# Attention and experts on one core: two of four steps of a root on ScalarE, three groups without float32 products, and a new order of tasks

## The chip, the cores and the metric

One NeuronCore of a Trainium2 chip runs the whole kernel; the other cores take no part. The metric is the device time of one execution in microseconds (us). A profile comes from one further execution, recorded by the hardware profiler: its span runs from the first to the last instruction and is a little shorter than that execution's device time.

## The reference, cut to what matters

Attention over 8 batches of 12 heads, 448 rows of 64, with normalised queries and keys; its output goes through a mixture of 8 experts with a router that places each token by sorted scores.

```python
rms = np.sqrt(np.mean(x * x, axis=-1, keepdims=True) + 1e-06)   # for q and for k
q_n, k_n = x / rms * g
scores = scale * np.matmul(q_n, k_n.transpose(0, 1, 3, 2))
attn = np.exp(scores - np.max(scores, axis=-1, keepdims=True))
attn = attn / (np.sum(attn, axis=-1, keepdims=True) + 1e-09)
x = np.matmul(attn, v)             # then tokens x 768
logits = x @ w_gate                # greedy: each token to one expert, 448 to an expert
h = np.maximum(x[mask] @ w1[e], 0.0)
out[mask] = h @ w2[e]
```

## The kernel before, in words

**Stages.** Attention comes first (to about 453 us of the profile), then the first search of the router (to about 486 us), then eight experts, whose products fill TensorE to the end. The change touches attention alone.

**Groups.** Four heads make a group, and there are 24 groups (g = 0 to 23). A group has seven blocks of query rows (d = 7 g + b, b = 0 to 6) for each of two halves. Two pairs of results (pair = 2 g + a) come out of a group, 48 in all; six pairs make a batch, which goes on to the router.

**One group's way through the engines.** ScalarE squares q and k (`sq`), VectorE sums the squares (`ss`), then comes the reciprocal square root of the sums (`r`): n = 1 is a logarithm and n = 2 an exponential on ScalarE, and n = 3 is one refinement by Newton's rule, y (y*y*ms - 192) in four small operations on GpSimd, lines 311 to 314, on 28 numbers a partition. Groups 0 and 1 refine on VectorE instead (lines 317 to 319). Then q and k are scaled by the root (`normk` on GpSimd, `normq` on ScalarE in 14 pieces), q is multiplied by the gains (`gain`, GpSimd), both are split in a high and a low float16 part (`hi` on ScalarE, `lo` on GpSimd), and a DMA transposes the parts (`trh`, `trl`).

TensorE then forms products for the row maxima (`max`, line 497), which VectorE reduces (`red`, line 506), and the scores (`score`, lines 528 and 530). ScalarE takes the exponential of a block of scores (`exp`, line 536, into e). TensorE multiplies e with the values (`av`, seven units a pair; the last of the seven in two halves).

**Wide and narrow blocks.** A block of e is either *wide*, one float32 product with the values in float32 (line 571), or *narrow*, three float16 products (lines 577, 579, 581), for which e's low part is first formed by `split` (line 552) on GpSimd, or on VectorE. `MIX` has a letter for each group: "4" has four wide blocks, "2" has two (b = 0 and 4, one in each pair), "0" none. `LO_POOL` names the blocks that are split on GpSimd.

**The end of a pair.** VectorE divides by the sums (`xn0`, `xn1`, `xn2`, lines 603 to 607) and writes the high and low parts (`xhi`, `xlo`, lines 623 to 629); only then is the pair's accumulator free, of which there are two. The logits of batches 0 to 6 are formed by `gate`, copied by `glo` (ScalarE) and added by `gsum` (VectorE); `early` is the first part of the router's work on them, 12 operations on VectorE (lines 1147 to 1187). The last batch is turned on TensorE (`xturn`, line 660, one for each of its pairs), copied out by ScalarE and VectorE (`xtd`, lines 673 and 675) and projected (`glast`), and `gcopy` (line 720) ends the stage.

**Order.** Every task goes to one engine (T TensorE, D VectorE, A ScalarE, P GpSimd, S the DMA queue of SyncE), and every engine works its tasks strictly in the order of the table `ORDER`, two characters a task. The numbers in `US` and the arguments on times and buffers serve the program that made the table and the check of its consistency; they set no order themselves.

## Time and profile before

| | us |
|---|---|
| three runs | 959.23, 955.66, 954.76 |
| median | 955.66 |
| profiled execution, device time | 961.13 |
| its span | 959.4 |
| busy in the span: PE, VectorE, ScalarE, GpSimd | 906.9, 692.6, 512.7, 459.6 |

PE is the name of TensorE in the profile, DVE of VectorE, ACT of ScalarE, POOL of GpSimd. Matmuls overlap in the engine's pipeline, so the busy time of PE says little of its load; the distance from one start to the next does. The profiled execution was 5.5 us longer than the median run.

### The profile page before, as it was taken

Reading aid. Unit: us, or ns where it says so; the run is one execution under the profiler, and the core shown is the slowest. Engines: PE = TensorE matmul, PEld = TensorE weight load, DVE = VectorE, ACT = ScalarE, POOL = GpSimd, SP = SyncE. Lnnn points to the kernel's source line nnn. Section 1 sums busy time; section 2 is a strip of 40 time slices with the busy share of each in tenths; the row PEclk is TensorE's granted clock in tenths of the full one; section 3 lists DMA queues with packets and bytes.
Section 4 is the critical chain, followed back from the end, with each engine's and each line's share of the span. In section 5 each row is a group of like instructions: output and inputs, shape, how many; then the busy total and the mean of one; then the engine's idle time right before and its main releaser. Section 6 shows DMA issues by size and latency. Waiting matters only on the chain.

```text
span 959.4 us, 24827 instructions
## 1 busy us (share of the span) xinstructions
PE 906.9 (95%) x10288; PEld 584.3 (61%) x10288; DVE 692.6 (72%) x1559; ACT 512.7 (53%) x945; POOL 459.6 (48%) x460
## 2 busy tenths in 40 slices
PE   2799999999999999998699999899999999999996
PEld 1367777676777677777466556455565565655553
DVE  6889999998999889884887787577876858234110
ACT  5889988888877888753052424233332424233111
POOL 7779999999988889873100302111112011110001
PEclk9989999999999999999599999999999999999999
DMA  7477889898997979571272919496866739583001
GB/s 190 116 141 144 206 170 207 167 211 156 235 199 168 161 183 167 127 151 60 87 236 90 322 47 243 147 252 185 240 173 212 208 135 285 166 176 124 30 17 42
DMA packets 264229, 157.72 MB, mean 164 GB/s; under 512 B 189876, under 2 KB 251316, under 8 KB 263092
## 3 DMA queue, kind: packets, MB, share of 16 engines
q1 hardware_dynamic: 258674, 133.66, 58.8%
q0 software_dynamic: 4608, 22.02, 7.0%
q8 instruction: 80, 1.31, 0.6%
q10 hardware_dynamic: 834, 0.46, 0.2%
q14 instruction: 33, 0.27, 0.1%
HBM read 94.42 MB, written 22.02 MB: 121 GB/s over the span
## 4 chain that ended last, share of the span: by engine, by line
issue 36%; PE 35%; POOL 14%; DVE 5%; DMA 4%; ACT 3%; POOLq 0%; SPq 0%; DVEq 0%; ACTq 0%
PE po L571 7%; PE psc L528 7%; PE ph L1669 6%; POOL pl L552 4%; PE pm L497 3%; POOL out_dram L1702 3%; POOL rows L1607 3%; PE py L1686 2%; POOL s L376 2%; PE psc L530 2%; DVE mx L506 2%; PE po L577 2%; PE po L581 2%; PE po L579 2%; DMA kq<-s 1%
## 5 line engine op out<-in xcount | busy, mean ns | idle before, releaser
L1669 PE MATMUL ph<-xt,w1h 128*128 128x448 f16 (+2 forms) x804 | 210.9, 345 | 4.1 <-DMA xt<-rows 3.4
L506 DVE TENSOR_REDUCE mx<-pm 128x2 f32<-128x896 f32 x162 | 176.0, 1087 | 29.3 <-PE pm L497 28.2
L552 POOL TENSOR_TENSOR pl<-e 128x896 f16<-128x896 f32 x102 | 174.0, 1722 | 20.0 <-ACT e L536 16.8
L1702 POOL DMA_INDIRECT out_dram<-y,idx x32 | 33.8, 1058 | 312.1 <-ACT y L1688 239.0
L571 PE MATMUL po<-v,e 128*128 128x65 f32 (+1 forms) x1056 | 174.7, 280 | 0.0
L536 ACT ACTIVATE e<-psc 128x896 f32<-128x896 f32 x168 | 147.8, 909 | 36.7 <-PE psc L530 35.6
L571 PEld LDWEIGHTS po<-v,e 128*128 128x128 f32 (+1 forms) x1056 | 132.8, 177 | 33.7 <-issue 31.9
L1669 PE MATMUL ph<-xt,w1l 128*128 128x448 f16 (+2 forms) x402 | 137.4, 345 | 0.0
L579 PE MATMUL po<-vs,e 128*128 128x64 f16 (+1 forms) x1008 | 130.0, 194 | 0.0
L528 PE MATMUL psc<-kq 64*128 64x448 f16 (+1 forms) x1152 | 127.6, 360 | 2.1 <-ACT e L536 1.4
L577 PE MATMUL po<-vs,e 128*128 128x65 f16 (+1 forms) x1008 | 129.3, 195 | 0.0
L581 PE MATMUL po<-vs,pl 128*128 128x65 f16 (+1 forms) x1008 | 128.5, 193 | 0.4 <-POOL pl L552 0.4
L1686 PE MATMUL py<-w2h,hh 128*128 128x384 f16 x384 | 125.0, 326 | 0.0
L1686 PE MATMUL py<-w2h,hl 128*128 128x384 f16 x384 | 125.0, 326 | 0.0
L1686 PE MATMUL py<-w2l,hh 128*128 128x384 f16 x384 | 125.0, 326 | 0.0
L1669 PEld LDWEIGHTS <-w1h 128*128 128x128 f16 x804 | 74.3, 98 | 65.3 <-issue 6.0
L1659 ACT ACTIVATE hh<-ph 128x448 f16<-128x448 f32 x64 | 34.8, 543 | 146.5 <-PE ph L1669 143.4
L577 PEld LDWEIGHTS <-e 128*128 128x128 bf16 (+1 forms) x1008 | 108.8, 123 | 0.0
L1686 PEld LDWEIGHTS <-hh 128*128 128x128 f16 x768 | 73.6, 97 | 45.8
L1688 ACT ACTIVATE y<-py 128x384 f32<-128x384 f32 x48 | 23.5, 490 | 132.8 <-PE py L1686 108.3
L1661 DVE SCALAR_TENSOR_TENSOR hl<-ph,hh 128x448 f16<-128x448 f32 x64 | 39.3, 619 | 71.2 <-ACT hh L1659 71.1
L1607 POOL DMA_INDIRECT rows<-xd,idx x32 | 31.5, 984 | 119.4 <-DVE idx L1504 50.6
(273 smaller groups left out, 1860.5 us busy)
## 6 DMA issues: line engine op xcount, KB each, us to landing
stage<-in_moe_w_dram SPq DMA_DIRECT2D x64, 768.0 KB
vraw<-in_v_dram SPq DMA_DIRECT2D x24, 384.0 KB
xd<-xa SPq DMA_DIRECT2D x8, 1152.0 KB
qkraw<-in_q_dram SPq DMA_DIRECT2D x11, 768.0 KB
qkraw<-in_k_dram SPq DMA_DIRECT2D x11, 768.0 KB
vraw<-in_v_dram SPq DMA_DIRECT2D x48, 32.0 KB
xd<-xa SPq DMA_DIRECT2D x16, 96.0 KB
qkraw<-in_q_dram SPq DMA_DIRECT2D x22, 64.0 KB
```

The lines of the kernel that those rows point to most:

```text
L506: self.nc.vector.tensor_reduce(m, p[r, :, :448], axis=AX.X, op=OP.max)
L528: mm(o, k[r, mine], q[r, all_], start=i == 0, stop=False)
L536: self.nc.scalar.activation(e, p[:, :, :448], AF.Exp, scale=scale)
L552: eng.tensor_tensor(l, self.T["e", d], self.T["ph", d], op=OP.subtract)
L571: nc.tensor.matmul(out, self.T["e", d][:, h, q0:q0 + m], self.v32[g % 2][:, 2 * h + a, wide.index(b % 4)], start=first, stop=last)
L577: nc.tensor.matmul(out, e[:, h, q0:q0 + m], vh, start=first, stop=False)
L579: nc.tensor.matmul(out[:, :64], e[:, h, q0:q0 + m], vl[:, :64], start=False, stop=False)
L581: nc.tensor.matmul(out, l[:, h, q0:q0 + m], vh, start=False, stop=last)
L1607: nc.gpsimd.indirect_dma_start(out=g[:n, c, :], out_offset=None, in_=self.xd, in_offset=bass.IndirectOffsetOnAxis(ap=idx[:n, c:c + 1], axi ...
L1669: nc.tensor.matmul(p, a, b[:, o], start=st, stop=sp)
L1686: nc.tensor.matmul(p, a[:, f, s], b[:, f, o], start=st, stop=sp)
L1702: st = nc.gpsimd.indirect_dma_start(out=self.out, out_offset=bass.IndirectOffsetOnAxis(ap=self.router.idx[k][:n, c:c + 1], axis=0), in_=y[ ...
```

## The change

The root's refinement (n = 3) becomes four tasks from group 2 on: n = 3 (a square) and n = 5 (minus 192) on ScalarE, n = 4 and n = 6 (the two products of tensors) on GpSimd. The last three groups have no wide block: all seven blocks are split, six on GpSimd (five before) and one, b = 4, on VectorE (none before), and `vfull`, the copy of their values in float32, goes. The table `ORDER` is another one throughout. A switch that would put `xn0` on ScalarE is added and stays on VectorE ("xn0" = "D"); the changed numbers in `US` and the changed `after` of `square` act on nothing that runs but through the table.

```diff
     WIDE = {"4": (0, 2, 4, 6), "2": (0, 4), "0": ()}
-    LO_POOL = {"4": (1, 3, 5), "2": (1, 2, 3, 5, 6), "0": (1, 3, 5)}
-    MIX = "444" + 6 * "422" + "222"
+    LO_POOL = {"4": (1, 3, 5), "2": (1, 2, 3, 5, 6), "0": (0, 1, 2, 3, 5, 6)}
+    MIX = "444" + 6 * "422" + "000"
...
+        elif a is None and self.engine("root", g) == "A":
+            if n == 3:
+                self.nc.scalar.activation(t, y, AF.Square)
+            elif n == 4:
+                self.nc.gpsimd.tensor_tensor(t, t, ms, op=OP.mult)
+            elif n == 5:
+                self.nc.scalar.activation(t, t, AF.Copy, bias=-192.0)
+            else:
+                self.nc.gpsimd.tensor_tensor(y, t, y, op=OP.mult)
         elif self.engine("root", g, a) == "P":
             P = self.nc.gpsimd
             P.tensor_tensor(t, y, y, op=OP.mult)
...
-    ENG = dict(lok="P", loq="P", normk="P", normq="A", gain="P", vfull="A", root="P", xhi="D")
+    ENG = dict(lok="P", loq="P", normk="P", normq="A", gain="P", vfull="A", root="A", xhi="D", xn0="D")
...
-                for n in range(1, 4):
-                    q = "A" if n < 3 else e("root")
-                    add("r", q, US["small" if n < 3 else "root" + q], self.rsqrt, g, n,
+                long = e("root") == "A"
+                for n in range(1, 7 if long else 4):
+                    q = "A" if n < 3 else "APAP"[n - 3] if long else e("root")
+                    add("r", q, US["small" if q == "A" else "tinyP" if long else "root" + q], self.rsqrt, g, n,
                         after=[("ss", g, 0), ("ss", g, 1)] if n == 1 else [("r", g, n - 1)], make=("r", g, n), uses=[("st", g)])
...
     ORDER = (
-        "06070n0u0z0809000m0o0y0w0v0+0-11120x13141s1R1S05101P1Q1v1t0115161u17031T1U1V18ZM04021z2L1+1w1x1-0A201A0r191C1E"
+        "060u0y07080905000v0w0z0+0-0n111202131R140m0o101516171s1u1S0x1O1P1x1Q031T1U191t1z181A1C1E2L1V1w1X1a1W1B1v1-1b1Y"
...
```

**The root of group 16.** On GpSimd the four steps of group 16 stood in a row before; L552 is a split, L376 a low part, L364 the gains:

```order
L552 TENSOR_TENSOR pl<-e 128x896 x2
L311 TENSOR_TENSOR st<-st 128x28
L312 TENSOR_TENSOR st<-st 128x28
L313 TENSOR_SCALAR st<-st 128x28
L314 TENSOR_TENSOR st<-st 128x28
L376 TENSOR_TENSOR s_4629<-qn,s_4629 128x896
```

Now two are left there, L313 (n = 4) and L317 (n = 6); the lines of the changed file are some nine higher, so that L561 is a split, L385 a low part, L373 the gains:

```order
L373 TENSOR_TENSOR qn<-qn,ggs 128x896
L313 TENSOR_TENSOR st<-st 128x28
L561 TENSOR_TENSOR pl<-e 128x896 x2
L385 TENSOR_TENSOR s_4737<-qn,s_4737 128x896
L317 TENSOR_TENSOR st<-st 128x28
```

On ScalarE, where the old table had only L306 and L308 (n = 1 and 2) of it, the changed program has L311 (n = 3) and L315 (n = 5) too; L545 is an exponential, L341 the norm of q:

```order
L306 ACTIVATE st<-st 128x28
L308 ACTIVATE st<-st 128x28
L545 ACTIVATE e<-psc 128x896
L311 ACTIVATE st<-st 128x28
L524 ACTIVATE qm_131<-mx 128x14
...
L382 ACTIVATE s_4737<-qn 128x896
L294 ACTIVATE sq_136<-qkraw 128x14x64
L294 ACTIVATE sq_137<-qkraw 128x14x64
L315 ACTIVATE st<-st 128x28
L545 ACTIVATE e<-psc 128x896 x2
L341 ACTIVATE qn<-qkraw,st 128x64 x14
```

Between the two products two splits and a low part are worked on GpSimd, and ten other tasks between the two steps on ScalarE. Of the 22 groups, 21 have such other work between n = 4 and n = 6 on GpSimd, from one split (group 11) to four splits and a low part (group 12); in group 10 nothing stands between.

**The start, on VectorE.** The sums of squares of group 2 (L300 with 128x14, the last two rows) stood behind three reductions of maxima and four copies of turned keys (L406) before:

```order
L319 SCALAR_TENSOR_TENSOR st<-st 128x4x3
L406 COPY kq<-po 128x384
L506 TENSOR_REDUCE mx<-pm 128x2
L406 COPY kq<-po 128x384
L506 TENSOR_REDUCE mx<-psc 64x2
L506 TENSOR_REDUCE mx<-psc 128x2
L406 COPY kq<-po 128x512 x2
L300 TENSOR_REDUCE st<-sq_136 128x14
L300 TENSOR_REDUCE st<-sq_137 128x14
```

In the changed program, from the same step on (the third of group 1's refinement), one reduction (L515) and two copies (L415) are ahead of the second of them:

```order
L328 SCALAR_TENSOR_TENSOR st<-st 128x4x3
L515 TENSOR_REDUCE mx<-psc 64x2
L415 COPY kq<-po 128x384
L300 TENSOR_REDUCE st<-sq_136 128x14
L415 COPY kq<-po 128x512
L300 TENSOR_REDUCE st<-sq_137 128x14
```

Both sums moved ahead of two reductions and two copies or more. On ScalarE n = 1, 2 and 3 of group 2 then follow one another, where before a copy of turned keys stood between n = 1 and n = 2.

**The end, on VectorE.** Before, `early` (its last two rows here, L1157 and L1187) was ahead of the last five pairs; the first of those, pair 43, follows:

```order
L1157 TENSOR_SCALAR key<-keyi 128x21
L1187 TENSOR_TENSOR cmp<-key,hit_80 128x672
L603 TENSOR_SCALAR z<-po 128x7
L605 RECIPROCAL z<-z 128x7
L607 TENSOR_TENSOR po<-po,z 128x7x64
```

Now it stands behind pairs 43 and 44 and ahead of pair 45, of the sum of batch 6's logits (L744, L745) and of the last split on VectorE (L561):

```order
L1172 TENSOR_SCALAR key<-keyi 128x21
L1202 TENSOR_TENSOR cmp<-key,hit_80 128x672
L615 TENSOR_SCALAR z<-po 128x7
L617 RECIPROCAL z<-z 128x7
L744 TENSOR_TENSOR logits<-po,lsc 128x24
L745 TENSOR_TENSOR logits<-po,lsc 64x8
L561 TENSOR_TENSOR pl<-e 128x896
L619 TENSOR_TENSOR po<-po,z 128x7x64
```

So two pairs are finished ahead of `early`, and three behind it. On TensorE the last three scores stood ahead of the last 21 units of `av` before, and all six `xturn` behind the last unit; now the last three scores are ahead of 14 units, and `xturn` 0 to 3 stand among those.

## Rows read from the trace of the kernel before

**Rows 1.** Busy time by stage: stretch, its length, each engine's busy us (instructions), clock, DMA.
```profile
60.00:317.00 257.00, 252.69 (x3937) 184.59 (x3934) 236.38 (x379) 218.52 (x471) 241.38 (x210) 1.00 0.87 180
...
404.00:446.00 42.00, 41.94 (x782) 32.62 (x782) 30.22 (x74) 18.75 (x26) 27.59 (x20) 1.00 0.47 100
```

**Rows 2.** Chain of waits, shares by line: first of 60:317, then of 317:446.
```profile
by line: POOL pl L552 15.2%; PE po L571 12.5%; PE psc L528 10.6%; POOL s L376 8.7%; issue 6.1%; DVE mx L506 5.2%; PE pm L497 5.2%; DMA kq<-s 4.9%; PE psc L530 3.3%; POOL kn L335 3.3%; POOL qn L364 2.6%; PE po L581 2.3%; PE po L577 2.2%; PE 
...
by line: PE po L571 28.0%; PE psc L528 25.6%; PE pm L497 8.3%; PE po L577 7.8%; PE psc L530 7.8%; PE po L581 7.7%; PE po L579 7.6%; DVE vs L468 2.0%; PE po L685 1.4%; PE po L686 0.9%; DVE mx L506 0.8%; issue 0.8%; PE po L692 0.7%; PE po L69
```

**Rows 3.** The same chain in order of time: start us, us, what.
```profile
316.76 0.20 PE po L581
...
445.23 0.27 PE po L571 x4
...
452.76 0.18 DVE logits L720
```

**Rows 4.** Timeline of PE: start us, us, line, operation, tiles, count.
```profile
399.82 0.41 PE L571 MATMUL po<-v,e 128*128 128x65 f32 x2
400.07 0.19 PE L577 MATMUL po<-vs,e 128*128 128x65 f16 x1
...
400.35 0.30 PE L571 MATMUL po<-v,e 128*128 128x65 f32 x1
```

**Rows 5.** POOL: groups of 60:317 (busy us, mean ns, idle before); timeline at 288 us.
```profile
L552 POOL TENSOR_TENSOR pl<-e 128x896 f16<-128x896 f32 x61 | 103.7, 1717 | 4.9 <-ACT e L536 4.1 <-DMA xd<-xa 0.4
...
L311 POOL TENSOR_TENSOR st<-st 128x28 f32<-128x28 f32 x15 | 3.9, 261 | 1.1 <-ACT st L308 1.1
...
288.38 0.23 POOL L311 TENSOR_TENSOR st<-st 128x28 f32<-128x28 f32 x1
...
289.52 1.89 POOL L376 TENSOR_TENSOR s<-qn,s 128x896 f16<-128x896 f32 x1
```

**Rows 6.** Two inputs in SBUF on DVE: timeline of one, and a group's mean.
```profile
14.62 0.90 DVE L376 TENSOR_TENSOR s<-kn,s 128x512 f16<-128x512 f32 x1
...
L468 DVE SCALAR_TENSOR_TENSOR vs<-vraw,vs 128x1024 f16<-128x1024 f32 x15 | 27.1, 1808 | 0.0
```

**Rows 7.** Timeline of DVE at the end: early, pairs 43, 44 and 47.
```profile
420.75 0.32 DVE L1147 TENSOR_REDUCE best<-logits 128x21 f32<-128x168 f32 x1
...
425.59 0.16 DVE L603 TENSOR_SCALAR z<-po 128x7 f32<-128x7 f32 x1
...
427.89 1.22 DVE L468 SCALAR_TENSOR_TENSOR vs<-vraw,vs 128x1024 f16<-128x1024 f32 x1
429.02 0.16 DVE L603 TENSOR_SCALAR z<-po 128x7 f32<-128x7 f32 x1
...
445.82 0.17 DVE L603 TENSOR_SCALAR z<-po 128x7 f32<-128x7 f32 x1 [1.33 <-PE po L581]
```

**Rows 8.** Timeline of ACT, two operations on 28 numbers a partition.
```profile
282.81 0.23 ACT L306 ACTIVATE st<-st 128x28 f32<-128x28 f32 x1 [1.78 <-DVE st L300]
283.07 0.23 ACT L308 ACTIVATE st<-st 128x28 f32<-128x28 f32 x1
```

**Rows 9.** Timeline of DVE and POOL at the start, before the root of group 2.
```profile
22.38 0.35 DVE L406 COPY kq<-po 128x384 f16<-128x384 f16 x1
...
26.57 2.09 DVE L300 TENSOR_REDUCE st<-sq 128x14 f32<-128x910 f32 x2
...
32.66 0.23 POOL L311 TENSOR_TENSOR st<-st 128x28 f32<-128x28 f32 x1 [4.46 <-ACT st L308]
```

**Rows 10.** Who waited for whom in the whole span: us in total, times, longest.
```profile
POOL pl L552 <- ACT e L536: 16.8, 13, 3.4
...
POOL st L311 <- ACT st L308: 6.7, 3, 4.5
...
ACT qn L332 <- POOL s L376: 2.9, 4, 1.1
```

More of the change, by code (lines that the diff above doesn't have):

```diff
@@ L602, in x_norm @@
         if n == 0:
-            V.tensor_scalar(z[:, 0], po[:, :, 64], 1e-9 * self.PSC, None, op0=OP.add)
+            if self.engine("xn0", pair) == "A":
+                self.nc.scalar.activation(z[:, 0], po[:, :, 64], AF.Copy, bias=1e-9 * self.PSC)
+            else:
+                V.tensor_scalar(z[:, 0], po[:, :, 64], 1e-9 * self.PSC, None, op0=OP.add)
         elif n == 1:
@@ L783, in plan @@
                 for i in range(2):
-                    add("sq", "A", US["copyA"], self.square, g, i, after=[("raw", g - g % 2, i)], make=("sq", g, i),
+                    add("sq", "A", US["copyA"], self.square, g, i, after=[("raw", g if g < 2 else g - g % 2, i)], make=("sq", g, i),
                         opens=[("sq", 2 * g + i)] + [("st", g)] * (1 - i), uses=[("raw", g // 2)] + [("st", g)] * i)
@@ L793, in plan @@
                     q = e("norm" + name)
-                    add("norm" + name, q, US["norm" + q], self.norm, g, i, after=[("r", g, 3)],
+                    add("norm" + name, q, US["norm" + q], self.norm, g, i, after=[("r", g, 6 if long else 3)],
                         make=(name + "n" if i else "qm", g), opens=[(name + "n", g)], uses=[("raw", g // 2), ("st", g)],
@@ L869, in plan @@
             b, hp = divmod(pair, 6)
-            add("xn0", "D", 0.17, self.x_norm, pair, 0, after=[("po", pair)], make=("z", pair),
+            e = self.engine("xn0", pair)
+            add("xn0", e, 0.17 if e == "D" else US["small"], self.x_norm, pair, 0, after=[("po", pair)], make=("z", pair),
                 opens=[("z", pair)] + [("xb", b)] * (hp == 0))
@@ L999 @@
[L999 to L1001 removed]
+        "060u0y07080905000v0w0z0+0-0n111202131R140m0o101516171s1u1S0x1O1P1x1Q031T1U191t1z181A1C1E2L1V1w1X1a1W1B1v1-1b1Y"
+        "1c1+2M2o2p2t1F1GDMDS2s20211Z1D1y2K22232NaR2O2P2QDN2q2u252r2RDODT2w242S2T3m0r0s1H1d1e26282U291J2W2v3K1I3q2x2y2z"
@@ L1002 @@
+        "a3aDaEaFaGaHaIaAaBaMaOaNZgZpa2a4aJaCZxaPaKaL"
     )
```

85 lines of the change are left out of this document (42 added, 43 removed).

## The prediction

> **What bounds the kernel now.** I read the stages first, then the chain of waits in two stretches, then single engines. After 486 us the program works the experts, which the change doesn't touch, so the question is when attention ends. No engine is idle for long before that. From 60 to 317 us, GpSimd is busy for 241.4 of 257 us (94%), VectorE for 236.4 (92%), ScalarE for 218.5 (85%) [rows 1]. The chain of that stretch runs over GpSimd's lines for 15.2 + 8.7 + 3.3 + 2.6 = 29.8%, over TensorE's for about as much again, and it changes hands often [rows 2]. From 317 on it is another kernel: the chain is on TensorE from 316.76 almost without a break to the last unit at 445.23, and the copy of the last logits, with which attention ends, starts at 452.76 [rows 2, 3], while GpSimd is busy for 27.6 of 42 us after 404 [rows 1]. So time is won in the last stretch by less work on TensorE, and before it by less work on GpSimd, as far as VectorE lets the rest go along.
>
> **The change part by part.**
>
> *Narrow blocks in the last three groups.* A float32 product holds TensorE from 399.82 to 400.07, 0.25 us; the nine float16 products of the three narrow blocks behind it hold it from 400.07 to 400.35, 0.28 us or 0.093 a block [rows 4]. A block made narrow saves 0.157 us. Three groups of two pairs of seven units have 42 such blocks; the six that are worked in halves I count at nothing. 36 x 0.157 = 5.65 us, all in the stretch that TensorE bounds: 2.8 in pairs 42 to 44, and 2.8 in pairs 45 to 47, which I count with the end below. Price: three more splits on GpSimd of 1.72 us each [rows 5] and three on VectorE. A split on VectorE isn't in the old trace. The nearest row is the same operation on 512 numbers, 0.90 us [rows 6], so 1.6 for 896; the lower bound is that row itself, 0.9, the upper 1.8, the mean of an operation on 1024 numbers [rows 6]. GpSimd has 14.4 us of idle time after 404 to cover its 5.2, VectorE 11.8 to cover 4.8 [rows 1]. Without that cover they would cost themselves. The three copies of values in float32 leave ScalarE, which is idle for more than half of that stretch, so for nothing.
>
> *The end.* From the start of pair 44's division at 429.02 [rows 7] to 452.76 it takes 23.7 us now. In the new order VectorE has to do in this stretch: pair 44 (2.3 us, as pair 43 from 425.59 to 427.89), `early` (420.75 to 425.59, 4.84) [rows 7], the first steps of 45, the sum of logits (0.3), a split (1.6), and the rest of 45, 46 and 47 (6.9): 15.9 us. Then follow turning, copying and projecting of what is left of the last batch. All six pairs of it now take from 445.82 + 2.3 = 448.1 to 452.76, 4.6 us; with four of six turned before I take 3.0 (1.5 to 4.6). Pair 46's first product now waits for the sum of logits behind `early`, since the two accumulators are taken; until then TensorE has the gates, pair 45 and five scores to do, so I add 1 us of waiting, no more. Sum 19.9 us, a gain of 3.8 (bounds 0, if a late split holds the last pair, and 7.0, without the wait, with 1.5 for the turning and 0.9 for the split). It contains the 2.8 of pairs 45 to 47.
>
> *Half of the root to ScalarE.* The four steps take GpSimd from 288.38 to 289.52, 1.14 us with the gaps between them [rows 5]. Two leave: 0.57 us. 15 of the 22 roots lie between 60 and 317 us [rows 5], 8.55 us of GpSimd's time; the others lie where GpSimd isn't in the chain. How much comes out in the end? At least nothing, at most all; by GpSimd's 30% of the chain it is 2.5, and I take that. ScalarE starts a second operation on 28 numbers 0.26 us after the first [rows 8], so it gets 15 x 2 x 0.26 = 7.8 us more in that stretch: 226 of 257, 88%, below both other engines. The Trainium skill advises against this move: "ScalarE: Activation LUTs", Rules for kernel authors, gives multiplying and adding to VectorE and tells to count some 0.3 us for each activation and 0.83 ns an element, an estimate of 0.32 us here and 9.7 us in that stretch. By it ScalarE would be at 89%, and the sum is the same; the trace has the shorter time. The root itself gets longer, since each of its steps now waits for the other engine: by the order, one split (1.7 us) to four splits and a low part (8.8 us) stand between its two products on GpSimd, in 21 of 22 groups. That work hides the hop from engine to engine; in group 10, where none stands, GpSimd waits for the operation on ScalarE at least, 0.26 us. What is queued behind a waiting n = 5 on ScalarE are exponentials, for which TensorE and GpSimd wait; that is the fourth case below.
>
> *The start.* GpSimd waits for 4.46 us before group 2's root at 32.66 [rows 9], which is the start of its steady work. In the old order, from 22.38 to the sums at 26.57, 4.2 us, VectorE works three reductions and four copies; one reduction and two copies stay, so the second sum comes some 2.5 us earlier, and no copy stands in ScalarE's way between n = 1 and 2. At most the whole wait is won, 4.5 us; at least nothing, if the later stages are bound by other things. I take 2.0.
>
> *Everything else in the order* moves loads, transposes and stores too. I find none moved that the chain of the old trace speaks of and cost that at nothing; the DMA of transposed keys has 4.9% of the chain [rows 2], 12.6 us, which is what is at stake if they come later.
>
> **Sum.** 2.8 + 3.8 + 2.5 + 2.0 = 11.1 us. The profiled execution had 961.13 us, so it would have 950.0. The median of the three runs is 5.5 us lower, 955.66; I take the same difference from it: **944.6 us**, 1.2% less.
>
> **The rivals.**
>
> *VectorE bounds the middle.* With 92% busy from 60 to 317 [rows 1], it may not be able to follow an earlier GpSimd. For it speaks that its share is nearly GpSimd's; against it, that VectorE's line has only 5.2% of the chain [rows 2]. Then the two terms of the start and the middle (4.5) are lost and the 6.6 of the last stretch stay: 949.1 us.
>
> *GpSimd takes TensorE's place in the last three groups.* It has 18 splits there, 18 x 1.72 = 31 us, and no other bulk to do than one group's low parts. They come at the pace of the exponentials, for which GpSimd waited 16.8 us in all [rows 10]. If they run late, TensorE waits, and the 6.6 are lost while 4.5 stay: 951.2 us. A split on VectorE may make it worse: an operation of the same class took 1.22 us at 427.89 [rows 7], in the stretch in which GpSimd is idle for a third of the time [rows 1], and 1.81 in the mean [rows 6]. The Trainium skill, "GPSIMD Engine Reference", Key points, says that GpSimd shares its way into SBUF with VectorE where an instruction of that has two inputs in SBUF; the two rows agree with it.
>
> *Slower: ScalarE stands before n = 5.* ScalarE works in order, so wherever GpSimd is late by one split (1.72 us), n = 5 holds up the exponentials behind it, and with two score buffers TensorE stops soon after. It decides from 11.1 / 1.72 = 6.5 groups on; in half of the 22 groups it costs 19 us, against the 11.1 won: 963.5 us. For it: the new waits are there in all 22 groups. Against it: ScalarE waited for GpSimd only 2.9 us in four places so far [rows 10], though the norm of q stood behind the root in the same way, and GpSimd waited 6.7 us for ScalarE's n = 2 in three places, most of it at the start.
>
> *All of it comes through.* If GpSimd's whole 8.55 and 4.5 us pass on to the end, the gain is 19.7 us: 936 us. The idle time of VectorE between 60 and 317, 20.6 us, would allow it.
>
> **How the numbers follow.** Chances: the forecast 0.48 (its own range is 940 to 949.5), VectorE bounds the middle 0.20, GpSimd bounds the last groups 0.10, slower 0.12, everything 0.10. A measurement of this kernel tells 0.5%, 4.8 us, from no change: faster means below 950.9, slower above 960.4. Faster are the forecast, all of the last case and seven tenths of the second case: 0.72. The same are the third case and the rest of the second, with some of the first: 0.16. Slower is 0.12. The range, 937 to 957, leaves out a part of the last case and most of the slow one.
>
> **What the profile of the changed kernel would show.** Right: the last copy of logits starts near 442; 96 fewer records of float32 products, and still an unbroken chain on TensorE to its last units; GpSimd has two small steps a root and little idle time in front of them; group 2's first long step on GpSimd starts about 4 us earlier; from pair 44's division to the last copy about 20 us. Wrong: waits of ScalarE for GpSimd of many us at the third or fourth step of the root with exponentials behind; TensorE waiting for splits in the last 40 us; or VectorE's share from 60 us on at 95% and more with its lines in the chain.

## The result, and the profile after

The changed kernel takes **964.2 us** (median of 5 runs, 961.5 to 966.9) against 955.7 before (5 runs, 954.5 to 959.2): the ratio is 1.0084, with a 95% interval of 1.006 to 1.0108. It is 8.5 us slower by the medians, outside the predicted range of 937 to 957. One execution in this study, of the changed kernel without loads, took 1439.7 us at a granted clock of 0.565 where its eleven others took 951 to 955, and its ratio leaves that one out.

The windows of the changed kernel, which answer to [rows 1]: us, then busy us (instructions) of PE, PEld (its weight loads), DVE, ACT and POOL, granted clock, DMA share, GB/s.

```profile
60.00:317.00 257.00, 246.87 (x3772) 177.05 (x3768) 228.26 (x364) 217.08 (x486) 229.60 (x175) 0.98 0.90 179
404.00:446.00 42.00, 41.31 (x870) 29.92 (x866) 37.60 (x67) 21.98 (x30) 37.25 (x25) 1.00 0.69 145
```

Between 60 and 317 us every engine did less than before: PE 5.8 us less, VectorE 8.1, ScalarE 1.4, GpSimd 11.8 (of which some 7 are the 30 steps of 0.21 to 0.26 us that left the root). None of these engines became fuller in the middle; all of them waited more. What grew is the last number but one, the share of the DMA engines: 0.87 to 0.90. It stands in [rows 1] too, and the prediction doesn't speak of it.

The chain of waits of the changed kernel says what was waited for: shares by line of 60:317 and the longest pieces there (start us, us, what), to be read against [rows 2].

```profile
by line: PE po L580 16.0%; PE psc L537 13.3%; DMA kq<-s 9.7%; DMA qkraw<-in_k_dram 6.8%; PE pm L506 6.0%; DVE mx L515 5.1%; issue 4.5%; PE psc L539 4.1%; PE po L586 3.1%; PE po L590 3.1%; PE po L588 3.1%; DVE st L300 2.6%; DVE vs L477 2.4%;
...
127.25 6.22 DMA kq<-s
194.07 5.25 DMA kq<-s
213.26 6.16 DMA kq<-s
235.87 7.86 DMA qkraw<-in_k_dram
249.33 9.66 DMA qkraw<-in_k_dram
```

GpSimd's splits, the first entry before (15.2%), are gone from the head of the list. In their place stand two transfers: the transposed keys (9.7%, 24.9 us; before 4.9%, 12.6 us) and the loads of k (6.8%, 17.5 us).

So the changed kernel gained first and lost later. The first exponential of group 4 starts 4.8 us earlier than before (before at 112.6 us), that of group 6 0.8 us later, of group 12 1.2, of group 17 11.9, of group 21 13.7 later; the last copy of logits is 8.9 us later. At the start and at the end the timelines show the following on GpSimd and VectorE (start us, us, engine, line, operation, tiles, idle time before it):

```profile
28.95 0.24 POOL L313 TENSOR_TENSOR st<-st 128x28 f32<-128x28 f32 x1 [0.52 <-ACT st L311]
...
31.57 1.69 POOL L344 TENSOR_TENSOR kn<-qkraw,st 128x896 f32<-128x896 f32 x1
...
432.58 5.02 POOL L561 TENSOR_TENSOR pl<-e 128x896 f16<-128x896 f32 x2 [1.14 <-ACT e L545]
```
```profile
439.48 0.17 DVE L615 TENSOR_SCALAR z<-po 128x7 f32<-128x7 f32 x1 [1.13 <-PE po L590]
...
455.49 0.17 DVE L615 TENSOR_SCALAR z<-po 128x7 f32<-128x7 f32 x1 [1.11 <-PE po L590]
...
461.67 0.18 DVE L732 COPY logits<-po 128x24 f32<-128x24 f32 x1 [2.16 <-PE po L719]
```

GpSimd's wait of 4.46 us ahead of group 2's root [rows 9] is 0.52 us now. From pair 44's division (439.48) to the last copy (461.67) it takes 22.2 us; before it took 23.7 [rows 7, 3].

One remark on the two profiles: behind the last copy of logits the execution of before took 506.6 us more (959.4 - 452.76), the changed one 502.1, and most other executions of this study 501 to 505 (two of them 507 and 508). The 4.5 us that the one profile of before is longer there are not the change's; the spans differ by 4.4, the ends of attention by 8.9, the medians by 8.5. In the profile of before TensorE stands for 3.37 us in the middle of the experts, and its granted clock is at half (1.2 GHz) for 3.4 us from 607.2 on; the profile of the changed kernel has neither there:

```profile
607.35 0.53 PE L1669 MATMUL ph<-xt,w1h 128*128 128x448 f16 x1 [3.37 <-DMA xt<-rows]
```

### The profile page after: what moved, and what is told of

Its sections match the earlier page's. It is cut to its first block, busy times and chain, and to the rows that moved or that the text cites. A ratio compares the mean times of both kernels' runs of the same rounds, so it can differ in the third digit from the quotient of the medians.

```text
span 963.8 us, 24918 instructions
## 1 busy us (share of the span) xinstructions
PE 903.1 (94%) x10335; PEld 578.7 (60%) x10336; DVE 703.5 (73%) x1562; ACT 517.0 (54%) x986; POOL 458.3 (48%) x419
## 4 chain that ended last, share of the span: by engine, by line
issue 36%; PE 32%; DVE 12%; POOL 7%; DMA 7%; ACT 4%; SPq 1%; POOLq 0%; ACTq 0%; DVEq 0%
PE po L580 6%; PE psc L537 6%; PE ph L1684 5%; DVE mx L515 4%; DMA kq<-s 3%; POOL rows L1622 3%; PE pm L506 3%; PE py L1701 2%; POOL out_dram L1717 2%; PE po L586 2%; PE po L590 2%; DVE st L300 2%; DMA qkraw<-in_k_dram 2%; PE po L588 2%; PE psc L539 2%
## 5 line engine op out<-in xcount | busy, mean ns | idle before, releaser
L515 DVE TENSOR_REDUCE mx<-pm 128x2 f32<-128x896 f32 x162 | 175.8, 1085 | 30.0 <-PE pm L506 28.9
L561 POOL TENSOR_TENSOR pl<-e 128x896 f16<-128x896 f32 x105 | 186.3, 1785 | 20.5 <-ACT e L545 19.1
L1717 POOL DMA_INDIRECT out_dram<-y,idx x32 | 33.1, 1036 | 312.0 <-ACT y L1703 239.0
L545 ACT ACTIVATE e<-psc 128x896 f32<-128x896 f32 x168 | 148.8, 910 | 44.5 <-PE psc L539 41.7
L580 PE MATMUL po<-v,e 128*128 128x65 f32 (+1 forms) x960 | 158.8, 281 | 0.4 <-DVE xa L641 0.2
L580 PEld LDWEIGHTS po<-v,e 128*128 128x128 f32 (+1 forms) x960 | 121.1, 178 | 36.6 <-issue 31.6
L588 PE MATMUL po<-vs,e 128*128 128x64 f16 (+1 forms) x1056 | 132.0, 195 | 0.1
L586 PE MATMUL po<-vs,e 128*128 128x65 f16 (+1 forms) x1056 | 131.5, 196 | 0.0
L590 PE MATMUL po<-vs,pl 128*128 128x65 f16 (+1 forms) x1056 | 130.6, 194 | 0.4 <-POOL pl L561 0.4
L586 PEld LDWEIGHTS <-e 128*128 128x128 bf16 (+1 forms) x1056 | 110.8, 121 | 2.1 <-issue 1.8
L590 PEld LDWEIGHTS <-pl 128*128 128x128 f16 (+1 forms) x1056 | 90.8, 102 | 0.8 <-POOL pl L561 0.6
```

The lines of the kernel that those rows point to most:

```text
L515: self.nc.vector.tensor_reduce(m, p[r, :, :448], axis=AX.X, op=OP.max)
L545: self.nc.scalar.activation(e, p[:, :, :448], AF.Exp, scale=scale)
L561: eng.tensor_tensor(l, self.T["e", d], self.T["ph", d], op=OP.subtract)
L580: nc.tensor.matmul(out, self.T["e", d][:, h, q0:q0 + m], self.v32[g % 2][:, 2 * h + a, wide.index(b % 4)], start=first, stop=last)
L586: nc.tensor.matmul(out, e[:, h, q0:q0 + m], vh, start=first, stop=False)
L588: nc.tensor.matmul(out[:, :64], e[:, h, q0:q0 + m], vl[:, :64], start=False, stop=False)
```

## The experiments

Lines of code are those of the changed kernel; a few kernels have them one to three lines further down. "Old" and "new" are the orders of before and of the changed kernel. Each time is a median with the ratio to runs of the kernel before on the same chip and its 95% interval. The theories were: **A**, the new order itself costs the time, by the loads and transposes in SyncE's queue; **B**, the split root makes the preparation of a group longer, so that buffers come free later; **C**, ScalarE stands before n = 5, the prediction's slower rival.

### Taking the change apart

*The whole root on GpSimd in the new order.*

```diff
-    ENG = dict(lok="P", loq="P", normk="P", normq="A", gain="P", vfull="A", root="A", xhi="D", xn0="D")
+    ENG = dict(lok="P", loq="P", normk="P", normq="A", gain="P", vfull="A", root="PPPPPPPPPPPPPPPPPPPPPPPP", xhi="D", xn0="D")
...
 GpSimd, group 14:   normk(13) split(68)
-                    r(14, n=4) gain(13) r(14, n=6) lok(13)
+                    r(14, n=3) gain(13) lok(13)
```

> The new order as it is, but the four steps of the root stay together on GpSimd, at the place where the new order has n = 4. Theory A (the new order of the middle itself costs the time, by loads and transposes that are issued later on SyncE's queue): still slower than before, 962 to 966 us. Theory B (the split of the root makes each group's preparation longer, so that the raw buffers come free later and the loads land later): the 13 us that groups 4 to 19 lose are gone and the gains of the start and the end remain, 948 to 953 us. Theory C (ScalarE stands before n = 5): as B, 948 to 953 us.

960.5 us, ratio 1.0058 (1.0041 to 1.0074). Between the two theories: by the runs most of the loss stays without the split root, and 3.7 us went with the split (2.5 by the ratios), though the two intervals overlap. The one profile divides it otherwise. In that execution, 960.87 us long, the last copy of logits is 0.5 us earlier than in the profile of before, and 9.4 earlier than in the changed kernel. Behind that copy it takes 506.7 us, where the changed kernel takes 502.1; there TensorE pauses in the experts, as in the profile of before:

```profile
452.23 0.18 DVE L732 COPY logits<-po 128x24 f32<-128x24 f32 x1 [1.84 <-PE po L719]
...
605.88 0.53 PE L1682 MATMUL ph<-xt,w1h 128*128 128x448 f16 x1 [2.86 <-DMA xt<-rows]
```

The six executions of this kernel took 959.4 to 963.2 us; whether the others lose their time in the experts too, one profile can't show. So how the loss divides between the order and the split stays open. That the gains of the start and the end, 8.6 us in the prediction without the root's, don't come out is plain either way.

*The split root in the old order.*

```diff
 GpSimd, group 14:   gain(13)
+                    r(14, n=4)
                     split(68)
-                    r(14, n=3)
+                    r(14, n=6)
```

> The old order and the old last groups, with the root in four tasks on ScalarE and GpSimd: n = 3 right behind n = 2, n = 6 at the place of the old root, n = 4 one task of GpSimd earlier, n = 5 between them. Theory A: 953.2 to 956 us (0 to 2.5 us gained, as the prediction had it for this part). Theories B and C: slower, 960 us or more; C with waits of ScalarE for GpSimd at n = 5 of many us, B with loads that land later and squares that wait for them.

1013.6 us, ratio 1.0606 (1.0591 to 1.0621), 58 us slower. But not as theory C has it. The waits of that kernel (engine, line, waited for, us in total, times, longest):

```profile
POOL st L317 <- ACT st L315: 65.3, 20, 8.7
...
POOL st L313 <- ACT st L311: 8.1, 3, 5.6
```

ScalarE never stands long before n = 5 (2.0 us in two places); GpSimd stands before n = 6, in 20 of 22 roots, 65 us in all, since n = 5 comes up in ScalarE's queue only behind the exponentials that stand ahead of it. The wait that the prediction feared is there, on the other engine and one step later. The new order is made for the split: in the changed kernel the same wait is 1.4 us in two places.

*The new start, the new end.* Both are spliced at a point where the two orders have done nearly the same tasks.

```diff
 new_start: ORDER up to the scores of group 4
-  old
+  new (roots of groups 2 to 8 split)
 new_end: ORDER from the scores of group 18 on
-  old, MIX = "444" + 6 * "422" + "222"
+  new, MIX = "444" + 6 * "422" + "000"
```

> The new order up to the scores of group 4 (with the split root in groups 2 to 8), and from there the old order, the old roots and the old last groups. In the changed kernel group 4 begins 4.8 us earlier than before. If the old middle carries a gain of the start to the end: 951 us. If the middle is bound by something that the start doesn't move (loads, VectorE): 954 to 956 us. Theory B: the split roots of groups 5 to 8 take the gain away again by group 8, 956 us or more.

959.2 us, ratio 1.0046 (1.0029 to 1.0063). Group 4 began 5.8 us earlier, group 5 1.2 later than before, and the last copy 0.5 later: the gain of the start was gone within 20 us, and the runs are 3.6 us slower in the median (the profile is of the fastest of the six, 956.99). In the stretch in which it goes, the chain of the changed kernel is on VectorE (here its shares from 114 to 134 us, with two pieces):

```profile
by line: DMA kq<-s 31.1%; DVE mx L515 17.9%; DVE vs L477 10.2%; DVE wg L190 7.7%; DVE xa L635 6.9%; DVE po L619 6.4%; issue 6.4%; DVE xa L640 4.6%; DVE st L300 3.7%; DVE z L617 2.1%; PE pm L506 1.8%; DVE wg L191 1.5%; DVE xa L641 1.3%; PE p
...
116.18 2.03 DVE vs L477
...
127.25 6.22 DMA kq<-s
```

VectorE works without a break from 113 to 127 us, and then a transfer of transposed keys takes 6.2 us.

> The old order up to the scores of group 18, and from there the new one, with the last three groups without float32 products and the split root in groups 22 and 23 only. By the prediction's own terms for the narrow blocks (2.8) and the end (3.8): 955.7 - 6.6 = 949 us. If GpSimd's splits run late in the last groups instead: 953 to 956 us.

958.7 us (952.2 to 964.5), ratio 1.0037 (1.0017 to 1.0057). 8 us are lost just behind the splice (group 19's exponentials: from 3.9 to 12.1 us later than before), 4.3 won back from group 21 to the last copy. The profile is of the slowest of the eleven executions, 964.5 us, and in it the granted clock is at half from 366.4 us on for 10.2 us, in the very stretch of the loss; so the 8 us are that execution's, and where the other executions lose their 3 us isn't shown.

*The narrow blocks alone, either way.*

```diff
 new_wide, old_narrow:
-    MIX = "444" + 6 * "422" + "000"
+    MIX = "444" + 6 * "422" + "222"
```

(The first is this on the changed kernel, with `vfull` behind `vhi` again; the second the reverse on the old one, six splits put in behind their exponentials as early as the seven buffers for low parts allow.)

> The changed kernel with two float32 blocks a group in the last three groups again (the six new splits dropped, three copies of the values in float32 put back on ScalarE). The prediction counts 5.65 us for these blocks: 969 to 970 us. From pair 40 to the last copy the changed kernel won back 0 to 5 us against the old one in the profiles; if the float32 products weren't what bounds the last 40 us: 963 to 965 us.

966.1 us, ratio 1.0112 (1.0086 to 1.0138): the float32 products cost 2 us by the medians, not 5.65, and the two intervals overlap, so that not even the 2 are shown.

> The old kernel with no float32 block in the last three groups; the six new splits stand as early as the order and the seven buffers allow. By the prediction's term: 950 to 951 us (5.65 us won). If the splits come too late in an order that wasn't made for them, GpSimd holds TensorE: 955 us or more, with waits of TensorE for the low parts after 404 us.

957.9 us, ratio 1.0026 (1.001 to 1.0043). No gain in an order that isn't made for it: from 396 to 450 us TensorE and its weight loads wait 2.9 and 3.2 us for the low parts, and GpSimd does four splits in 7.6 us without a pause at 428.8.

*One step of the root alone on ScalarE.*

```diff
-                    q = "A" if n < 3 else "APAP"[n - 3] if long else e("root")
+                    q = "A" if n < 3 else "APPP"[n - 3] if long else e("root")
...
             elif n == 5:
-                self.nc.scalar.activation(t, t, AF.Copy, bias=-192.0)
+                self.nc.gpsimd.tensor_scalar(t, t, 1.0, -192.0, op0=OP.mult, op1=OP.add)
```

> The old kernel with one step of the root's refinement moved: the square goes to ScalarE right behind n = 2, the three other steps stay together on GpSimd at the place of the old root, so nothing comes back from ScalarE to GpSimd. By the prediction's way of counting, 15 x 0.28 us = 4.2 us of GpSimd's time between 60 and 317 us, of which 30% come out: 954.5 us. By the run with the root in four tasks in the old order (58 us slower), if the way from GpSimd to ScalarE and back is what cost there: no loss here, 954 to 956 us. If any further step on ScalarE in this order costs: 960 us or more.

958.2 us, ratio 1.0028 (1.0003 to 1.0052): neither. Without the way back the 58 us are gone, but taking a step from GpSimd brings nothing; the kernel is a little slower, just clear of noise.

### SyncE's queue

*One queue in the other order.* The two orders around the loads of group 14 in SyncE's queue:

```
old: trm(8) lv(8,1) lqk(14,0) lqk(14,2) rows(8) lqk(14,5) trh(10) xtr(1,3) lqk(14,1)
new: xtr(1,3) trl(9) rows(8) trh(10) lqk(14,0) lqk(14,2) lqk(14,1) trm(9) lqk(14,3)
```

The first large load of groups 14 and 15 stands ahead of both transposes of group 10 in the old queue, and in the new one behind the first of them (`trh`) and ahead of the second; the same holds for the pairs that begin with groups 12, 16 and 18, one transpose later each time.

```diff
 new_old_sp: the five engines in the new order
-  SyncE's queue new
+  SyncE's queue old
 old_new_sp: the five engines in the old order
-  SyncE's queue old
+  SyncE's queue new from task 37 on
```

> The new order on all engines but SyncE, whose queue (loads, transposes, stores) is worked in the old order. Theory A1 (the new order costs the time through SyncE's queue: transposes stand ahead of loads that come late): most of what the changed kernel has lost after group 4 comes back, 954 to 959 us. Theory A2 (the new order of the five other engines costs it, and late loads are only what follows): 962 us or more. The root is split as in the changed kernel, which by the run with whole roots costs 3.7 us.

> The old kernel, but SyncE's queue is worked in the new order from its 37th task on (before that it can't be done in this order). Theory A1: 959 us or more, with squares that wait for loads. Theory A2: 954.5 to 957 us.

1016.5 us (1.0631, 1.0587 to 1.0674) and 1022.5 us (1.0717, 1.0681 to 1.0752). By the letter each theory is met once (A2 by the first run, A1 by the second, both of which said "or more") and missed once; neither expected 60 us. A queue in an order that doesn't go with the others costs that much, whichever of the two it is. That says how much hangs on this queue, not which order is better.

*Without the loads.*

```diff
     def load_qk(self, g, n):
+        if g >= 8:
+            self.T["raw", g // 2] = self.T["raw", g // 2 - 2]
+            return
         if n == 0 and g != 1:
```

> The changed kernel without the loads of q and k from group 8 on: groups 8 to 23 square and scale the q and k of groups 4 to 7 once more, so the output is not the reference's; all tasks on the five other engines stay, and 48 DMA issues leave SyncE's queue. If late loads are what the changed kernel loses in its middle (7.9 and 9.7 us of loads stand in its chain between 235 and 259 us): 954 to 958 us. If the loads are late only because everything else is: 962 us or more.

> The old kernel with the same loads left out, to tell what the loads cost in an order that has them in time: 953 to 956 us, since its chain waits for a load of q once, 2.9 us, and hardly at all after group 8.

953.3 us (0.9975, 0.9961 to 0.9989) and 954.3 us (0.9985, 0.9971 to 1.0). This is the first answer: without the loads the new order gets 10.9 us faster, the old one 1.5. **The whole loss is there only with the loads of q and k**, and what is left of the change's gain is 1 us, inside the intervals.

*The root late.*

```diff
 GpSimd, group 14:   normk(13) split(68)
-                    r(14, n=3) gain(13) lok(13)
+                    gain(13) r(14, n=3) lok(13)
```

> The new order with the whole root on GpSimd, now at the place of n = 6 (one to four splits later than in the run that had it at the place of n = 4, which took 960.5 us). If the split root costs because the root is finished later: as the changed kernel, 963 to 965 us. If it costs by the passing to and fro between the two engines, or by ScalarE's share: as the run with the early whole root, 959 to 962 us.

965.3 us, ratio 1.0111 (1.0076 to 1.0146), against 960.5 with the early whole root (1.0041 to 1.0074): as the changed kernel; the two intervals are just apart. So a root that is finished later is enough to cost what the split costs, without any passing to and fro. The profiles agree: the last copy of logits is at 452.2 us with the early whole root, at 458.3 with the late one, at 461.7 with the split. The loads show what hangs on it. There are two raw buffers for q and k, and the first load of a pair of groups waits for the norms of the pair before last (that of groups 18 and 19 for the norm of q of group 15, which ends at 248.84 in the changed kernel and at 237.64 before); in SyncE's queue the first load of group 18 is issued at 248.9 us in the changed kernel, at 246.4 with the early root and at 237.7 before; that of group 22 at 325.3, 318.3 and 317.4.

*Loads without waits, squares without waits, loads with an eighth of the bytes.*

```diff
 new_loads_apart, from group 8 on:
-        src, t = (self.q, self.k)[i], self.T["raw", g // 2][:, i]
+        src, t = (self.q, self.k)[i], self.T["raw", 2][:, i]      # all engines read buffer 3
 new_squares_free, from group 8 on:
-        self.nc.scalar.activation(t, self.raw(g, i, a), AF.Square)
+        self.nc.scalar.activation(t, self.ggs.rearrange("p (h b d) -> p h b d", h=2, b=7), AF.Square)
 new_small_loads, from group 8 on (and no new raw buffer is taken):
-        self._load(self.dma_queue(self.load_queue(g, n)), src, t, g, r, slice(0, 4 if g == 1 else 8))
+        self._load(self.dma_queue(self.load_queue(g, n)), src, t, g, r, slice(0, 4 if g == 1 else 1))
```

> The changed kernel with all its loads of q and k in SyncE's queue, but from group 8 on they go to a buffer that nobody reads, and groups 8 to 23 use the q and k of groups 6 and 7 (the output is not the reference's). The loads cost their issue and their traffic as before; what is gone is that a load waits for the norms of four groups earlier and that squares and norms wait for the load. If it is these waits that cost the changed kernel its time: 953 to 956 us, as without the loads. If it is the 48 issues and their traffic in the queue: 961 us or more.

957.7 us, ratio 1.0021 (1.0004 to 1.0039): between the two. 6.4 of the 10.9 us come back when the waits go and the traffic stays. The other 4.4 come back when the traffic goes as well (953.3, intervals apart).

> The changed kernel, but from group 8 on the squares are taken of the spread gains, which are always there, in place of q and k (the output is not the reference's). Loads still wait for the norms of four groups earlier and norms still wait for the loads; only the squares no longer do. If the loads cost by squares that start late: 954 to 957 us. If they cost by what stands behind a waiting load in SyncE's queue (transposes of keys): 961 us or more.

962.5 us, ratio 1.008 (1.0059 to 1.0102): 1.6 us less than the changed kernel, not told from nothing. Squares that wait are not the way.

> The changed kernel with the same loads of q and k in the same places of SyncE's queue, but from group 8 on each of the 16 large ones (768 KB) brings an eighth of its bytes, 96 KB, the rest stays what an earlier group left (the output is not the reference's). Issues and waits are those of the changed kernel; only the traffic is less. With the loads in an unread buffer, which has all the traffic and none of the waits, it took 957.7 us, without the loads 953.3. If the DMA engines' load is the resource that the new order ran into (they are busy for all of the stretch from 110 to 160 us and for 95% from 235 to 317): 953 to 957 us. If it is the waits of the queue for the norms: 961 us or more.

953.4 us, ratio 0.9969 (0.9954 to 0.9984): the same issues at the same places, and **all of the loss is gone with seven eighths of the large loads' bytes**. The waits are not quite the same, against what was expected. The eighth that is left goes to the first group of a pair alone, and so the load no longer waits for the norms of the second. In the changed kernel all eight first loads from group 8 on start behind the end of the norm of q of the second group (here group 17, then the load for groups 20 and 21):

```profile
281.36 3.44 ACT L341 ACTIVATE qn<-qkraw,st 128x64 f32<-128x64 f32 x14
284.86 0.42 SPq L244 DMA_DIRECT2D qkraw<-in_q_dram  x1
```

With the small loads five of the eight start 0.2 to 2.9 us before that end:

```profile
273.28 3.44 ACT L343 ACTIVATE qn<-qkraw,st 128x64 f32<-128x64 f32 x14
273.86 1.13 SPq L244 DMA_DIRECT2D qkraw<-in_q_dram  x1
```

So this run takes away most of the traffic and a part of the waits, and the 10.7 us are the most that the bytes can have. The windows of the kernels show the traffic: the share of the DMA engines, the last number but one, in the old kernel, the changed one, the one with unread loads and the one with small loads, from 110 to 160 and from 235 to 317 us.

```profile
110.00:160.00 50.00, 49.46 (x794) 35.48 (x793) 46.88 (x77) 42.77 (x92) 49.00 (x38) 1.00 0.94 199
235.00:317.00 82.00, 80.02 (x1326) 59.39 (x1325) 75.14 (x123) 66.05 (x143) 73.26 (x58) 1.00 0.91 194
```
```profile
110.00:160.00 50.00, 47.75 (x767) 34.17 (x766) 43.44 (x73) 36.93 (x79) 42.24 (x30) 0.97 1.00 195
235.00:317.00 82.00, 75.15 (x1190) 53.90 (x1188) 69.30 (x110) 63.91 (x139) 70.31 (x63) 0.96 0.95 186
```
```profile
110.00:160.00 50.00, 47.07 (x746) 33.55 (x744) 42.63 (x71) 35.11 (x75) 40.36 (x30) 0.93 0.97 191
235.00:317.00 82.00, 78.01 (x1284) 56.53 (x1285) 74.88 (x118) 68.45 (x149) 75.81 (x66) 1.00 0.94 197
```
```profile
110.00:160.00 50.00, 49.39 (x820) 36.51 (x816) 46.74 (x79) 40.47 (x90) 45.37 (x32) 1.00 0.78 164
235.00:317.00 82.00, 79.75 (x1288) 58.71 (x1284) 75.95 (x117) 69.93 (x158) 75.67 (x66) 1.00 0.76 154
```

From 110 to 160 us the DMA engines of the changed kernel are busy all the time, and in both stretches every other engine does less than in the old kernel. With the small loads the DMA engines are at 0.78 and 0.76, and from 235 to 317 PE, VectorE and GpSimd are back at the old kernel's load or near it.

*The whole root with small loads.* The last two edits together.

> The new order with the whole root on GpSimd at the place of n = 4, and the large loads of q and k from group 8 on cut to an eighth (the output is not the reference's). With full loads the whole root was 3.7 us faster than the split one. If the split root costs only through the raw buffers that come free later and the loads behind them: no difference to the split root with small loads, 952 to 955 us. If it costs on the engines themselves: 949 to 951 us.

956.2 us, ratio 1.0004 (0.9988 to 1.0019), against 953.4 (0.9954 to 0.9984) for the split root with small loads. Neither expected value: once the DMA engines have room, the split root is 2.8 us **faster**, and the intervals are just apart. The window of 235:317 with the whole root shows GpSimd at 79.95 of 82 us, 97.5%:

```profile
235.00:317.00 82.00, 79.49 (x1284) 57.42 (x1281) 72.29 (x120) 69.72 (x151) 79.95 (x74) 1.00 0.76 157
```

With the split it was 75.67, 92% (above). So the move does what it says on the engines, and with full loads its later finish takes that away again, by the medians more than that.

### Two tries at a faster kernel

*Norms early*, on the new order with the early whole root:

```diff
 GpSimd, group 14:   loq(13)
+                    normk(14)
                     split(72) split(73)
-                    normk(14)
 ScalarE, group 14 (loq(13) stands on GpSimd):
+                    normq(14)
                     exp(72) exp(73) sq(15) exp(74) exp(75) exp(76)
-                    normq(14)
```

> The new order with the whole root on GpSimd at the place of n = 4 (960.5 us), and in groups 8 to 21 the two norms, which give the raw buffer of q and k free, as early behind the root as the buffers allow: on GpSimd past up to three splits, on ScalarE past up to six exponentials. If late norms are why the loads are late: 955 to 959 us. If the exponentials and splits that now wait behind the norms cost as much: 960 us or more.

1031.9 us, ratio 1.0798 (1.0776 to 1.082). The waits of that kernel from 100 to 460 us:

```profile
POOL pl L561 <- ACT e L545: 76.7, 27, 7.2
...
PE psc L537 <- ACT e L545: 44.6, 11, 6.7
ACT qn L341 <- POOL s L385: 30.0, 11, 4.8
```

ScalarE stood 30 us before norms of q, until GpSimd's low parts (L385) were done, with exponentials behind. The second half of the expectation, many times over; whether late norms are the first cause of late loads can't be told this way.

*The change over one group later*: the splice of new_end at the scores of group 20, all roots whole.

> The old order up to the scores of group 20 (one group later than in the run that changed over at group 18) and from there the new one, with the last three groups without float32 products and all roots whole on GpSimd. Where the run that changed over at group 18 lost 8 us at the seam, it won back 4.3 us from group 21 to the last copy; if that gain is the new end's own: 951 to 954 us, faster than both kernels. If each seam costs what it brings: 956 us or more.

955.1 us against 956.6, ratio 0.9987 (0.997 to 1.0004): 1.2 us by the ratio, which isn't told from no change. It is the best kernel of the study that computes everything; none is shown to beat the kernel before.

## Why the prediction was wrong

**What bounds the kernel: failed.** The prediction read the engines from [rows 1] and found GpSimd at 94% and VectorE at 92%. The DMA engines stood in the same row with 0.87, and stretch by stretch they were at 0.94 and 0.91 in the old kernel (above). In those stretches GpSimd was busy for 98% and 89%, so they were about as full. Room won on GpSimd came out as time only where they had room too (the runs with small loads).

**"Everything else in the order ... I find none moved that the chain of the old trace speaks of and cost that at nothing": this is the step that failed.** Its price, together with the root's later finish, was 10.9 us (964.2 to 953.3 us without the loads), where the old order paid 1.5 for the loads. And the order before the run showed it: the first large load of four of the pairs of groups stands behind one transpose more. The 12.6 us named there "what is at stake" became 24.9, and 17.5 us of loads came on top. How it works, as far as the traces tell: the norms of a group are later, the raw buffer comes free later, the load starts later and meets full DMA engines, so it lands later still (7.9 and 9.7 us in the chain), and the next transpose of keys starts only then (259.00). In SyncE's queue of the changed kernel this reads as follows (start us, us, line, operation, tiles):

```profile
245.09 2.00 SPq L394 DMA_TRANSPOSE kq<-s  x1
247.20 1.05 SPq L282 DMA_DIRECT2D vraw<-in_v_dram  x1
248.90 0.37 SPq L244 DMA_DIRECT2D qkraw<-in_q_dram  x1
249.33 0.57 SPq L244 DMA_DIRECT2D qkraw<-in_k_dram  x1
249.95 2.72 SPq L236 DMA_DIRECT2D qkraw<-in_q_dram  x1
...
259.00 1.60 SPq L394 DMA_TRANSPOSE kq<-s  x1
```

The old kernel issued the load of 248.90 at 237.70, and the load of k that goes with it 9 us later, not 0.4:

```profile
237.70 0.37 SPq L244 DMA_DIRECT2D qkraw<-in_q_dram  x1
...
246.69 0.58 SPq L244 DMA_DIRECT2D qkraw<-in_k_dram  x1
```

The runs tell these quantities: 10.9 us with the loads and all that hangs on them; 6.4 with the waits alone; 4.4 more with the traffic when the waits are gone; 10.7 with most of the traffic and a part of the waits. The two are not independent: a late load costs little when the DMA engines have room. That the 4.4 us are transposes that go slower beside the loads is argued, not shown. The Trainium skill, "DMA: Bandwidth & Descriptors", Bandwidth, has 6.15 us for 1 MB from HBM into SBUF, issued from GpSimd, an estimate of 4.6 us for one of these 768 KB, which SyncE issues. No run here has such a load by itself. The rows in the chain are 1.7 and 2.1 times the estimate; the second, of 249.33, has the load of q with as many bytes 0.43 us ahead of it.

**Half of the root, 2.5 us:** right in size where the DMA engines have room (2.8 us with small loads). With full loads the split is 3.7 us slower by the medians, intervals overlapping, and 9.4 later at the end of attention in the profiles; the gain isn't there, and a loss is likely but not shown. The prediction covered the hop with "that work hides the hop"; it did hide it, but nobody asked what the later finish of the root makes late next. It was the norms, the raw buffers and the loads.

**The start, 2.0 us:** the wait of 4.46 us is gone, group 4 starts 4.8 us earlier, and nothing of it reaches the end; with the new start alone the kernel is 0.46% slower. The chain says VectorE and then the transposed keys. The first rival, that VectorE bounds the middle, has the place right for these 14 us; over the whole stretch from 60 to 317 VectorE is busy for 89%, not for the 95% named as its sign. In the kernel without loads the lead doesn't get lost: there group 6 starts 3.7 us and group 16 6.5 us earlier than in the old kernel.

**Narrow blocks and the end, 2.8 + 3.8 us:** mis-sized. With float32 products put back the changed kernel is 2 us slower, and the splice with the new end is 1.2 us faster, neither told from nothing. From pair 44's division on it takes 22.2 us, not 19.9. From 404 to 446 us GpSimd is busy for 37.25 of 42 us and VectorE for 37.60: the idle time that should cover the new splits is nearly used up (the prediction's own sums were 32.8 and 35.0). Two splits at 432.58 took 5.02 us together, where the price was 1.72 each, and the split that VectorE has beside them took 2.56, where 1.6 was taken and 1.8 was the upper bound (the two others took 1.09 and 1.07):

```profile
433.50 2.56 DVE L561 TENSOR_TENSOR pl<-e 128x896 f16<-128x896 f32 x1
```

The prediction named the reason, operations on the two engines that lengthen one another, under its rivals and left it out of its price. And from the last pair's division, 455.49, it is 6.2 us to the last copy, 3.9 after its 2.3, where 3.0 was taken. The rival of GpSimd in TensorE's place was in part true: GpSimd's splits have 6.1% of the chain from 404 to 446 us, which is 2.6 us, and none of the main entries before.

**The slower rival:** its time, 963.5 us, was nearly the result, its mechanism not. ScalarE waited for GpSimd at n = 5 once, 1.3 us. That the hop can stop the kernel was shown in the old order, where GpSimd waits 65 us for n = 5.

**In sum**, the terms of 11.1 us came to about 1 us (953.3 against 954.3 with the loads out of the way on both sides, not told from nothing), and what was set at nothing cost about 9. How much of the 9 is the order's and how much the late root's stays open, since runs and profiles divide it differently (above). Where the rest of the gain is without loads stays open: in that kernel's profile the last copy of logits is 3.6 us earlier than in the old order without loads (4.75 against 1.12 us ahead of before), the medians say 1.0.

## What to carry to other kernels

Count the DMA engines among the engines: where their busy share in a stretch is as high as that of the fullest engine, a new order of tasks is also a new order of transfers, and a load that comes later has to be priced. When a short operation is put off because other work hides the wait, follow its result to the buffer that it gives free and to the load that waits for this buffer. Where every queue is worked strictly in order, the orders fit one another: of the parts that were taken over alone here, none won anything that can be told, and three cost 58 to 66 us. And look where in the span one profile loses its time before a difference of medians is put down to a stage.

## What the runs showed of the hardware that was not expected

- Fuller DMA engines moved no more: from 110 to 160 us the share is 1.00 at 195 GB/s in the changed kernel, 0.94 at 199 GB/s in the old. Most of the packets are small there (changed kernel):

```profile
DMA packets 23760, 9.76 MB, mean 195 GB/s; under 512 B 18558, under 2 KB 23624, under 8 KB 23624
```

- A pause of TensorE can be paid twice. In the changed kernel TensorE stood for 2.07 us up to 133.5 us, and from 134.5 on the granted clock was at half (1.2 GHz) for 3.4 us; the same came at 247.1 and 312.0 us behind pauses of 1.85 and 2.26 us. The windows show it as 0.97 and 0.96. The old kernel has no such stretch between 62 us and the end of attention. It is no rule: a pause of 1.58 us up to 276.6 in the same profile and one of 1.81 us with small loads (up to 268.5) were followed by none, and the splice with the new end fell to half for 10.2 us at 366.4 with no single pause over 1.2 us before it.
- The same split on GpSimd took 1.68 us at 429.68 and 2.51 on the mean of the two at 432.58, in one profile. What stands beside it on VectorE tells them apart: `vs` (L468 and L477) or a split, which read two inputs in SBUF. In the profiles of before and of the changed kernel together, 171 splits on GpSimd have neither beside them, and none of these took over 1.77 us. Of the 36 that have one, 19 took 1.9 to 2.7 us, and in all 19 the operation on VectorE had started first; in 14 of the 17 others, which took 1.7 to 1.8, the split had. At 421 us the split on GpSimd starts second, by 0.03 us, and is the longer one:

```profile
421.07 1.09 DVE L561 TENSOR_TENSOR pl<-e 128x896 f16<-128x896 f32 x1
421.10 2.61 POOL L561 TENSOR_TENSOR pl<-e 128x896 f16<-128x896 f32 x1
```
